# Folding the inverse transform of modes 0 to 31 into x early, and running the rest of the inverse on row halves

## The chip, the cores and the metric

The kernel runs on one core of a Trainium2 chip. The metric is device time in microseconds (us) of one execution. In its first measurement the kernel before took 431.39 us (median of 3 runs, 431.38 to 431.8).

## The reference, cut to what matters

```python
# linear attention, elu+1 features; x is (8, 576, 512)
x = attention(q, k, v)
X = rfft(x, axis=1)[:, :64]                     # 64 modes
Yr = Xr @ w_r[m] - Xi @ w_i[m]                  # per mode m: two 512x512 weight matrices
Yi = Xr @ w_i[m] + Xi @ w_r[m]
u = x + irfft(Y, n=576, axis=1)
out = u + relu(u @ w_ch)
```

The weights are 128 matrices of 1 MB (float32). They are cast to bfloat16 while they are loaded, so 512 KB of each lands on the chip. Because of the relu no row of the output can be finished before the last mode is known.

## The kernel before

After the attention, the kernel streams the weights through eight buffers and multiplies mode by mode. Between the modes it computes `x @ w_ch` for 36 tiles of 128 rows (`E0`). Near the end it turns the mode results `YT` into rows: for each batch entry `b`, `YZ[b]` holds the 112 rows of modes 0 to 55 (real and imaginary), once as they are (half 0) and once multiplied by `w_ch` (half 1).

```python
def form_rows(b):                       # called for two b after each of modes 55 to 58
    for ec in range(NDC):
        nc.tensor.matmul(z_ps[: 2 * NE, :], lhs[ec], wch16[:, ec, :], start=..., stop=...)
    for ec in range(NDC):
        nc.tensor.transpose(y_ps[: 2 * NE, ec, :], lhs[ec], id16)
    ...                                 # copied to YZ[b][:112, 1], YZ[b][:112, 0]

# mode_product(kk), kk >= 60: fillers keep TensorE busy
    if t == 1 and kk >= NM - 4: keep_warm(6)      # between the w_r and the w_i product
    if NM - 4 <= kk < NM - 1:   keep_warm(3)      # twice more; last_mode has keep_warm(3)

# the rows of modes 56 to 63 come last: one tile `last`, copied into each YZ[b] by DMA
for b in (1, 2, 3, 4, 5, 6, 7, 0):
    eng = nc.sync if b in (1, 2) else nc.gpsimd
    eng.dma_start(out=YZ[b][2 * NE : 128, :, :], in_=last[b::B, :, :])
```

The last stage works on 18 pairs of tiles. For each pair `channels` copies `E0` into PSUM (where the results of matmuls add up) with an identity matmul, `rectified` adds the inverse of half 1 and applies relu on ScalarE, and `finish` adds the inverse of half 0, after which VectorE adds x and sync issues the store. Each of these steps is one 512-column matmul per tile, six per pair, and the inverse contracts over all 128 rows (64 modes times two):

```python
mm(acc[r, :], inv_sb[:, sel], YZ[b][:, half, :])
...
for n in range(4, len(pairs)):
    channels(n); rectified(n); finish(n - 1)
```

## Time and profile before

| | before |
|---|---|
| time, median of 3 | 431.39 us |
| span of the profiled execution, first to last instruction | 429.8 us |
| last product of the last mode ends | 395.65 us |
| first store issued | 400.34 us |
| last VectorE add ends | 424.57 us |

The page of the kernel before, its busy times and three of its rows in 40 slices (each slice is 10.7 us):

```profile
PE 296.9 (69%) x2551; PEld 154.8 (36%) x2551; DVE 181.9 (42%) x373; ACT 146.6 (34%) x227; POOL 91.5 (21%) x165
...
PEclk9999666565558765566556678555658655999998
DMA  8999999999999999999999999999999999995697
GB/s 148 207 208 209 209 210 210 211 214 215 222 211 214 215 213 214 214 214 214 213 213 214 214 213 214 213 214 214 213 213 214 214 214 214 214 213 97 239 369 296
```

The DMA row is at 9 in nearly every slice. The bytes per second are those written on chip or to memory, near 213 GB/s while the weights stream. The windows view of the kernel before follows; its columns are the stretch in us, its length, the busy time of each engine with the number of instructions, the granted TensorE clock, the mean share of the 16 DMA engines, and GB/s:

```profile
core 0: us, PE busy (x) PEld busy (x) DVE busy (x) ACT busy (x) POOL busy (x), PEclk, DMA share, GB/s
300.00:350.00 50.00, 35.85 (x260) 14.13 (x259) 14.86 (x40) 12.31 (x22) 11.09 (x21) 0.64 1.06 213
...
390.00:395.00 5.00, 4.95 (x44) 2.23 (x44) 1.31 (x2) 0.00 (x0) 0.00 (x0) 1.00 0.41 76
...
400.00:404.00 4.00, 3.81 (x18) 1.79 (x17) 3.04 (x4) 2.40 (x6) 1.03 (x3) 1.00 0.63 222
404.00:408.00 4.00, 4.00 (x23) 1.96 (x22) 3.79 (x4) 3.20 (x7) 0.00 (x0) 1.00 0.89 359
408.00:412.00 4.00, 4.00 (x20) 1.68 (x20) 3.31 (x4) 2.98 (x7) 0.00 (x0) 1.00 0.91 370
412.00:416.00 4.00, 4.00 (x20) 2.05 (x19) 3.79 (x4) 3.33 (x7) 0.00 (x0) 1.00 0.98 382
...
420.00:424.00 4.00, 2.75 (x14) 0.85 (x12) 3.41 (x5) 2.04 (x4) 0.00 (x0) 1.00 1.02 408
424.00:428.00 4.00, 0.00 (x0) 0.00 (x0) 0.57 (x1) 0.00 (x0) 0.00 (x0) 0.71 0.81 297
```

In the weight phase the DMA share is 1.06 and TensorE is 72% busy. From 390 us the stream runs out. In the tail, 404 to 420 us, TensorE is busy for 4.00 of 4.00 us, VectorE for 3.3 to 3.8, and the stores move 359 to 382 GB/s. One pair of tiles in the timeline of the kernel before (start, length, engine, line, operation, count):

```profile
415.03 0.59 PE L593 MATMUL acc<-E,id 128*128 128x512 f16 x2
...
415.46 1.03 PE L549 MATMUL acc<-YZ,inv_sb 128*128 128x512 f16 x4
415.88 1.07 ACT L604 ACTIVATE acc<-acc 128x512 f32<-128x512 f32 x2 [0.22 <-PE acc L549]
...
416.32 0.59 PE L593 MATMUL acc<-E,id 128*128 128x512 f16 x2
```

From one pair to the next it is 1.29 us, six matmuls of 0.216 us. Line 593 is `channels`, line 549 the inverse, line 604 the relu.

### The profile page before, as it was taken

The page shows a single profiled execution, that of the slowest core. Times are in us where ns is not written, and L with a number is a line of the kernel's source. Part 1 is how long each engine was busy: PE and PEld are TensorE (multiplying, and loading weights), DVE is VectorE, ACT ScalarE, POOL GpSimd, SP SyncE. Part 2 cuts the span into 40 slices and gives each one's busy share as a digit, 9 for nine tenths or more (in the row PEclk, how much of TensorE's full clock was granted, in tenths as well). Part 3 has the DMA queues.
Part 4 walks back from the last instruction along what each step waited for, and adds up shares of the span by engine and source line. Part 5 has one row for each costly group of instructions (what it writes and reads, how often), then busy time and mean ns, then how long its engine had stood idle before and what let it go on. Part 6 is the DMA issues. An engine that isn't in the chain of part 4 may idle for free.

```text
span 429.8 us, 6238 instructions
## 1 busy us (share of the span) xinstructions
PE 296.9 (69%) x2551; PEld 154.8 (36%) x2551; DVE 181.9 (42%) x373; ACT 146.6 (34%) x227; POOL 91.5 (21%) x165
## 2 busy tenths in 40 slices
PE   0358776887018776856886666778675758999993
PEld 0346555664003332322232222322222324954441
DVE  1699998955004233233232322332323322211694
ACT  3687666631002222222222322122212222311782
POOL 4232223222102312121112221221211121110200
PEclk9999666565558765566556678555658655999998
DMA  8999999999999999999999999999999999995697
GB/s 148 207 208 209 209 210 210 211 214 215 222 211 214 215 213 214 214 214 214 213 213 214 214 213 214 213 214 214 213 213 214 214 214 214 214 213 97 239 369 296
DMA packets 35803, 92.38 MB, mean 215 GB/s; under 512 B 3136, under 2 KB 16448, under 8 KB 35776
## 3 DMA queue, kind: packets, MB, share of 16 engines
q0 software_dynamic: 32000, 82.00, 98.2%
q1 hardware_dynamic: 3776, 10.00, 6.1%
q8 instruction: 20, 0.33, 0.3%
q14 instruction: 7, 0.06, 0.0%
HBM read 164.07 MB, written 9.44 MB: 404 GB/s over the span
## 4 chain that ended last, share of the span: by engine, by line
DMA 67%; PE 17%; issue 7%; DVE 4%; ACT 2%; POOL 1%; DVEq 0%; POOLq 0%; ACTq 0%
DMA wi<-in_moe_w_i_dram 33%; DMA wr<-in_moe_w_r_dram 22%; DMA k<-in_k_dram 11%; PE acc L549 4%; PE P L355 3%; PE z L530 2%; PE zl L340 2%; PE acc L593 2%; PE eps L507 2%; PE yp L534 1%; DVE x L272 1%; ACT ke L187 1%; DVE k L194 0%; ACT qT L223 0%; POOL q L169 0%
## 5 line engine op out<-in xcount | busy, mean ns | idle before, releaser
L507 PE MATMUL eps<-wch,xTw 128*128 128x512 f16 x144 | 62.3, 582 | 3.4 <-DVE xTw L504 3.1
L515 ACT CAST E<-eps 128x512 f16<-128x512 f32 (+1 forms) x40 | 21.3, 543 | 122.7 <-PE eps L507 122.7
L115 POOL DMA_DIRECT2D wr<-in_moe_w_r_dram x64 | 34.0, 531 | 135.5 <-PE P L355 109.4
L355 PE MATMUL P<-wi,xt_c 128*32 128x512 bf16 x252 | 42.1, 565 | 27.3 <-DMA wi<-in_moe_w_i_dram 27.3
L355 PE MATMUL P<-wr,xt_c 128*32 128x512 bf16 x252 | 42.6, 582 | 22.9 <-DMA wr<-in_moe_w_r_dram 20.9
L115 POOL DMA_DIRECT2D wi<-in_moe_w_i_dram x65 | 34.5, 531 | 108.5 <-PE P L355 74.1
L355 PEld LDWEIGHTS <-xt_c 128*32 128x32 bf16 x504 | 24.3, 163 | 67.8 <-issue 38.7
L369 DVE CAST ys<-P 128x512 f16<-128x512 f32 x32 | 22.0, 688 | 59.7 <-PE P L355 59.7
L151 PEld LDWEIGHTS <-qT 64*128 64x128 f16 (+1 forms) x640 | 21.5, 126 | 56.8 <-issue 41.8
L371 ACT CAST ys<-P 128x512 f16<-128x512 f32 x31 | 18.1, 585 | 63.2 <-PE P L355 63.0
L373 PE MATMUL yt<-pick_sb,ys 128*128 128x16 f16 x252 | 16.8, 177 | 31.6 <-DMA pick_sb<-row_pick 20.4
L504 DVE COPY xTw<-xTp 128x512 f16<-128x512 f16 x36 | 15.2, 423 | 51.8 <-PE xTp L502 51.8
L373 PEld LDWEIGHTS <-ys 128*128 128x128 f16 x252 | 12.3, 105 | 51.1 <-issue 23.4
L151 PE MATMUL num<-kv,qT 64*128 64x65 f16 (+1 forms) x320 | 14.0, 230 | 22.6 <-ACT kv L247 20.1
L507 PEld LDWEIGHTS <-xTw 128*128 128x128 f16 x144 | 14.7, 124 | 33.7 <-issue 24.2
L492 DVE TENSOR_TENSOR x_main<-nw,rd 128x256 f32<-128x256 f32 x32 | 12.1, 419 | 33.8 <-PE nw L151 33.7
L187 ACT ACTIVATE qe<-q 128x1152 f16<-128x1152 f16 x16 | 17.7, 1155 | 22.9 <-DMA q<-in_q_dram 22.9
L216 PE MATMUL qTp<-id,qe 128*128 128x128 f16 x144 | 16.6, 310 | 12.1 <-DVE qe L200 11.7
L499 ACT CAST x16w<-x_main 128x512 f16<-128x512 f32 x32 | 19.8, 619 | 14.2 <-DVE x_main L492 14.2
L272 DVE TENSOR_TENSOR x<-num,rd 128x512 f16<-128x512 f32 x32 | 22.1, 691 | 1.1
L491 DVE RECIPROCAL rdw<-nw 128x4 f32<-128x4 f32 (+1 forms) x40 | 5.5, 170 | 38.3 <-PE nw L151 38.2
L502 PE MATMUL xTp<-id,x16w 128*128 128x128 f16 x144 | 19.4, 278 | 2.8 <-ACT x16w L499 2.4
(71 smaller groups left out, 413.7 us busy)
## 6 DMA issues: line engine op xcount, KB each, us to landing
wr<-in_moe_w_r_dram POOLq DMA_DIRECT2D x64, 512.0 KB, 18.6
wi<-in_moe_w_i_dram POOLq DMA_DIRECT2D x63, 512.0 KB, 18.6
out_dram<-x_main SPq DMA_DIRECT2D x14, 512.0 KB, 3.1
q<-in_q_dram POOLq DMA_DIRECT2D x8, 576.0 KB, 13.5
k<-in_k_dram POOLq DMA_DIRECT2D x8, 576.0 KB, 14.7
v<-in_v_dram POOLq DMA_DIRECT2D x8, 576.0 KB, 16.9
out_dram<-x_main SPq DMA_DIRECT2D x4, 256.0 KB, 3.4
out_dram<-x_tail SPq DMA_DIRECT2D x2, 512.0 KB, 3.4
```

Of the source, the lines that this page charges most:

```text
L115: tc.keep_in_program_order(nc.gpsimd.dma_start(out=w[:, dcs], in_=rows_of[:, dcs, :]))
L151: mm = nc.tensor.matmul(num[hpo][orow, c0 : c0 + 65], qT[rows, hpp, h2, cols], kv_sb[rows, hpp, h2, :])
L187: pin(nc.scalar.activation(out=ev[:, c], in_=heads(nm, b)[:, c], func=AF.Exp))
L272: nc.vector.tensor_tensor(out=dst.rearrange("p (o c d) -> p o c d", o=2, c=4), in0=nv[:, :, :, 0:64], in1=rden.unsqueeze(3).broadcast_to([ ...
L355: mm = nc.tensor.matmul(P[i][dc * 32 : dc * 32 + 32, :], xt_cols(dc, t, kk), w[:, dc, i * pw : i * pw + pw], start=(t == 1), stop=(t == 0) ...
L369: nc.vector.tensor_copy(out=dst, in_=P[i])
L371: nc.scalar.copy(out=dst, in_=P[i])
L373: mm = nc.tensor.matmul(yt_ps[:, ec, kk % 8, :], st[:, ec * 128 : ec * 128 + 128], pick_sb)
L499: nc.scalar.copy(out=x16, in_=x)
L502: nc.tensor.transpose(xT_ps[:, c, :], x16[:, c * 128 : c * 128 + 128], id16)
L507: nc.tensor.matmul(e_ps, xT[:, c, :], wch16[:, c, :], start=(c == 0), stop=(c == NDC - 1))
L515: nc.scalar.copy(out=dst, in_=e_ps[:, cols])
```

## The change

Its intent is to take a third of TensorE's work out of the last stage. The inverse of modes 0 to 31 is added to x earlier, in modes 32 to 55, before `x @ w_ch` is computed. So the last stage has only modes 32 to 63 to add, 64 rows instead of 128. These 64 rows are kept twice, in rows 0 to 63 and in rows 64 to 127, so that the two tiles of a pair can use different row halves of the array at the same time. The rows of modes 56 to 63 must then be copied into both halves: sixteen small DMA copies instead of eight. One constant that was loaded (144 KB) is built on the chip instead. The fillers of the last modes were set anew. The core of the diff:

```diff
+    FILL = {61: (2, 2, 1), 62: (5, 3, 3), 63: (6,)}
...
-            if t == 1 and kk >= NM - 4:
-                keep_warm(6)
-        if NM - 4 <= kk < NM - 1:
-            keep_warm(3)
+            if t == 1:
+                work_slot(kk, 0)
+                keep_warm(fill[0])
...
-    nc.sync.dma_start(out=inv0_sb, in_=inv0_dr.ap())
 (inv0_sb and inv2_sb, which holds modes 32 to 63 in both row halves, are built by selection matmuls)
...
+    def fold(t: int):                  # modes 32 to 55, pinned, with turn_x and channel_product
+                    acc[orow, :], inv_sb[: 2 * NF, rows_of(jj, BASE[b % 2])], YE[b][: 2 * NF, :]
+        pin(nc.vector.tensor_tensor(out=x, in0=acc, in1=x, op=ALU.add))
...
+    def form_z(b: int):                # spread over modes 56 to 60; form_y likewise
+            for h in range(2):
+                        z_ps[HALVES[h], :], yt, wch16[:, ec, :],
...
+                if n < N_PRE:
+                    mm(i, orow, inv0_sb[:, sel_rows], last[:, half, :])
+                else:
+                    g = HALVES[i]
+                    mm(i, orow, inv2_sb[g, sel_rows], YZ[b][g, half, :])
...
-        eng.dma_start(out=YZ[b][2 * NE : 128, :, :], in_=last[b::B, :, :])
+        for h in range(2):
+            eng.dma_start(out=YZ[b][64 * h + 48 : 64 * h + 64, :, :], in_=last[b::B, :, :])
```

More of the change, by code (lines that the diff above doesn't have):

```diff
@@ L18, with _dft_consts @@
 NP = 64
-def _dft_consts(S: int, NM: int, NL: int, NB: int):
+def _dft_consts(S: int, NM: int):
     m = np.arange(NM)
@@ L37, in _dft_consts @@
             pick[quad * 32 + c, c] = 1.0
-    inv0 = np.zeros((NL, 2, NB, S), dtype=np.float64)
-    inv0[:, :, 0, :] = inv[NM - NL :]
-    return (
-        fwd.astype(np.float16), inv.reshape(2 * NM, S).astype(np.float16),
-        inv0.reshape(2 * NL * NB, S).astype(np.float16), pick,
-    )
+    return fwd.astype(np.float16), inv.reshape(2 * NM, S).astype(np.float16), pick
 @with_exitstack
@@ L70 @@
     NE = NM - NL
-    fwd_np, inv_np, inv0_np, pick_np = _dft_consts(S, NM, NL, B)
+    NF = NM // 2
+    fwd_np, inv_np, pick_np = _dft_consts(S, NM)
     id16_dr = nc.inline_tensor(np.eye(128, dtype=np.float16), name="ident16")
@@ L75 @@
     inv_dr = nc.inline_tensor(inv_np, name="dft_inv")
-    inv0_dr = nc.inline_tensor(inv0_np, name="dft_inv_first")
     pick_dr = nc.inline_tensor(pick_np, name="row_pick")
@@ L345, in mode_product @@
         st = stage.tile([128, D], F16, tag="ystage", bufs=2, name=f"ys{kk}")
-        n_part = 1
-        pw = D // n_part
-        P = [
-            ps.tile([128, D], F32, tag="P", bufs=2, name=f"P{kk}_{i}")[:, 0:pw] for i in range(n_part)
-        ]
-        for t, w in ((1, wr), (0, wi)):
-            for i in range(n_part):
-                for dc in range(NDC):
-                    mm = nc.tensor.matmul(
-                        P[i][dc * 32 : dc * 32 + 32, :], xt_cols(dc, t, kk),
-                        w[:, dc, i * pw : i * pw + pw],
+        fixed = pin if kk >= NF else (lambda ins: ins)
@@ L358, in mode_product @@
+        fill = FILL.get(kk, (0, 0, 0))
+        P = ps.tile([128, D], F32, tag="P", bufs=2, name=f"P{kk}")
+        for t, w in ((1, wr), (0, wi)):
+            for dc in range(NDC):
+                fixed(
+                    nc.tensor.matmul(
+                        P[dc * 32 : dc * 32 + 32, :], xt_cols(dc, t, kk), w[:, dc, :],
                         start=(t == 1), stop=(t == 0), tile_position=(0, dc * 32),
                     )
-                    if kk >= NM - 4:
-                        pin(mm)
@@ L362, in mode_product @@
-            if t == 1 and kk >= NM - 4:
-                keep_warm(6)
-        if NM - 4 <= kk < NM - 1:
-            keep_warm(3)
-        for i in range(n_part):
-            dst = st[:, i * pw : i * pw + pw]
-            if (kk + i) % 2 == 0:
-                nc.vector.tensor_copy(out=dst, in_=P[i])
-            else:
-                nc.scalar.copy(out=dst, in_=P[i])
+                )
+            if t == 1:
+                work_slot(kk, 0)
+                keep_warm(fill[0])
+        if kk % 2 == 0:
+            fixed(nc.vector.tensor_copy(out=st, in_=P))
+        else:
+            fixed(nc.scalar.copy(out=st, in_=P))
@@ L372, in mode_product @@
+        work_slot(kk, 1)
+        keep_warm(fill[1])
         for ec in range(NDC):
-            mm = nc.tensor.matmul(
-                yt_ps[:, ec, kk % 8, :], st[:, ec * 128 : ec * 128 + 128], pick_sb
-            )
-            if kk >= NM - 4:
-                pin(mm)
-        if NM - 4 <= kk < NM - 1:
-            keep_warm(3)
+            fixed(
+                nc.tensor.matmul(
+                    yt_ps[:, ec, kk % 8, :], st[:, ec * 128 : ec * 128 + 128], pick_sb
+                )
+            )
@@ L381, in last_mode, with work_slot @@
+        keep_warm(fill[2])
+    work: list = []
+    per_slot: dict[int, list] = {}
+    def work_slot(kk: int, slot: int):
+        for _ in range(per_slot[kk][slot] if kk in per_slot else 0):
+            if work:
+                work.pop(0)()
     def last_mode(ps):
@@ L400, in last_mode @@
         product(1, wr, range(NDC))
-        keep_warm(3)
+        keep_warm(FILL[kk][0])
         product(0, wi, range(3))
@@ L421 @@
     inv_sb = ystage.tile([2 * NM, S], F16, name="inv_sb")
+    inv2_sb = ystage.tile([128, S], F16, name="inv2_sb")
     inv0_sb = ystage.tile([128, S], F16, name="inv0_sb")
+    sel = ystage.tile([128, 2, 128], F16, name="row_sel")
     nc.sync.dma_start(out=inv_sb, in_=inv_dr.ap())
-    nc.sync.dma_start(out=inv0_sb, in_=inv0_dr.ap())
+    nc.vector.memset(sel, 0.0)
+    for h in range(2):
+        nc.vector.tensor_copy(out=sel[:, 0, h * 64 : h * 64 + 64], in_=id16[:, 2 * NF : 128])
+    nc.vector.tensor_copy(out=sel[:, 1, 0:128:B], in_=id16[:, 2 * NE : 128])
     YT = ystage.tile([128, NDC, NM, 2 * B], F16, name="YT")
+    nc.vector.memset(YT[:, :, NE:NM, :], 0.0)
     yt_ps = None
@@ L436, in mode @@
         if kk == NM - 2:
-            nc.vector.tensor_copy(out=YT[:, :, NE : NM - 1, :], in_=yt_ps[:, :, 0 : NL - 1, :])
+            pin(nc.vector.tensor_copy(out=YT[:, :, NE : NM - 1, :], in_=yt_ps[:, :, 0 : NL - 1, :]))
         elif kk % 8 == 7:
-            nc.vector.tensor_copy(out=YT[:, :, kk - 7 : kk + 1, :], in_=yt_ps)
+            ins = nc.vector.tensor_copy(out=YT[:, :, kk - 7 : kk + 1, :], in_=yt_ps)
+            if kk >= NF:
+                pin(ins)
     for kk in range(n_early):
@@ L450 @@
     YZ = [sW.tile([128, 2, D], F16, tag="YZ", bufs=B, name=f"YZ{b}") for b in range(B)]
+    YE: dict[int, object] = {}
     E0: dict[int, object] = {}
@@ L473, with parts_of, attention_rows @@
     last_ps = []
-    def channel_product(t: int):
-        num = [bank(f"nw{t}_{o}") for o in range(2)]
-        tail = t >= B * NJJ
-        if tail:
-            i = t - B * NJJ
-            parts = [(2 * i + h, NJJ, slice(h * 64, h * 64 + 64)) for h in range(2)]
-        else:
-            parts = [(t // NJJ, t % NJJ, slice(0, 128))]
+    for i, dst in enumerate((inv2_sb, inv0_sb)):
+        for cols in (slice(0, 512), slice(512, S)):
+            r_ps = bank(f"rows{i}_{cols.start}")[:, 0 : cols.stop - cols.start]
+            nc.tensor.matmul(r_ps, sel[:, i, :], inv_sb[:, cols])
+            nc.scalar.copy(out=dst[:, cols], in_=r_ps)
+    def parts_of(t: int):
+        if t < B * NJJ:
+            b, jj = divmod(t, NJJ)
+            return [(b, jj, slice(0, 128))]
+        p = t - B * NJJ
+        return [(2 * p + h, NJJ, HALVES[h]) for h in range(2)]
+    def attention_rows(t: int):
+        num = [bank(f"nw{t}_{o}") for o in range(2)]
         x = x_of(t)
-        for b, jj, orow in parts:
+        for b, jj, orow in parts_of(t):
             nv = num_matmuls(num, orow, q_view(qT_all[b]), kv_all[b], rows_of(jj, BASE[b % 2]))
@@ L494, in channel_product, with early_rows @@
                     in0=nv[o][:, :, 0:64],
-                    in1=rden.unsqueeze(2).broadcast_to([64 if tail else 128, 4, Dh]),
+                    in1=rden.unsqueeze(2).broadcast_to([orow.stop - orow.start, 4, Dh]),
                     op=ALU.mult,
                 )
-        x16 = sW.tile([128, D], F16, tag="x16w", bufs=2, name=f"x16w{t}")
-        nc.scalar.copy(out=x16, in_=x)
+    def early_rows(b: int):
+        r = 2 * NF
+        y_ps = bank(f"ye{b}", [128, NDC, 128], F16)
+        for ec in range(NDC):
+            yt = YT[:, ec, 0:NF, :].rearrange("p m (t b) -> p (m t) b", b=B)[:, :, b]
+            pin(nc.tensor.transpose(y_ps[:r, ec, :], yt, id16))
+        YE[b] = sW.tile([128, D], F16, tag="YE", bufs=2, name=f"YE{b}")
+        pin(nc.vector.tensor_copy(out=YE[b][:r], in_=y_ps[:r].rearrange("p c r -> p (c r)")))
@@ new lines @@
+    x16w, xTw = {}, {}
+    def fold(t: int):
+        x = x_of(t)
+        acc = bank(f"ya{t}")
+        for b, jj, orow in parts_of(t):
+            pin(
+                nc.tensor.matmul(
+                    acc[orow, :], inv_sb[: 2 * NF, rows_of(jj, BASE[b % 2])], YE[b][: 2 * NF, :]
+                )
+            )
+        pin(nc.vector.tensor_tensor(out=x, in0=acc, in1=x, op=ALU.add))
+        x16w[t] = sW.tile([128, D], F16, tag="x16w", bufs=2, name=f"x16w{t}")
+        pin(nc.scalar.copy(out=x16w[t], in_=x))
@@ L500, in channel_product, with turn_x @@
+    def turn_x(t: int):
+        x16 = x16w.pop(t)
         xT_ps = bank(f"xTp{t}", [128, NDC, 128], F16)
         for c in range(NDC):
-            nc.tensor.transpose(xT_ps[:, c, :], x16[:, c * 128 : c * 128 + 128], id16)
-        xT = sW.tile([128, NDC, 128], F16, tag="xTw", bufs=2, name=f"xTw{t}")
-        nc.vector.tensor_copy(out=xT, in_=xT_ps)
+            pin(nc.tensor.transpose(xT_ps[:, c, :], x16[:, c * 128 : c * 128 + 128], id16))
+        xTw[t] = sW.tile([128, NDC, 128], F16, tag="xTw", bufs=2, name=f"xTw{t}")
+        pin(nc.vector.tensor_copy(out=xTw[t], in_=xT_ps))
@@ L505, in channel_product @@
+    def channel_product(t: int):
+        xT = xTw.pop(t)
         e_ps = bank(f"eps{t}")
         for c in range(NDC):
-            nc.tensor.matmul(
-                e_ps, xT[:, c, :], wch16[:, c, :], start=(c == 0), stop=(c == NDC - 1)
-            )
-        need = {t // NJJ} if not tail else {2 * i, 2 * i + 1}
-        for b in sorted(need):
+            pin(
+                nc.tensor.matmul(
+                    e_ps, xT[:, c, :], wch16[:, c, :], start=(c == 0), stop=(c == NDC - 1)
+                )
+            )
+        for b, _, _ in parts_of(t):
@@ L514, in channel_product @@
         for cols, dst in e0_parts(t):
-            nc.scalar.copy(out=dst, in_=e_ps[:, cols])
+            pin(nc.scalar.copy(out=dst, in_=e_ps[:, cols]))
     tiles = []
@@ L520 @@
         tiles += [(2 * i + 1) * NJJ + jj for jj in range(NJJ)]
-    def form_rows(b: int):
+    def form_z(b: int):
         z_ps = bank(f"z{b}")
+        for ec in range(NDC):
+            yt = YT[:, ec, NF:NM, :].rearrange("p m (t b) -> p (m t) b", b=B)[:, :, b]
+            for h in range(2):
+                pin(
+                    nc.tensor.matmul(
+                        z_ps[HALVES[h], :], yt, wch16[:, ec, :],
+                        start=(ec == 0), stop=(ec == NDC - 1), skip_group_check=True,
+                    )
+                )
+        pin(nc.scalar.copy(out=YZ[b][:, 1, :], in_=z_ps))
@@ L525, in form_rows, with form_y @@
+    def form_y(b: int):
         y_ps = bank(f"yp{b}", [128, NDC, 128], F16)
-        lhs = [
-            YT[:, ec, 0:NE, :].rearrange("p m (t b) -> p (m t) b", b=B)[:, :, b] for ec in range(NDC)
-        ]
         for ec in range(NDC):
+            yt = YT[:, ec, NF:NM, :].rearrange("p m (t b) -> p (m t) b", b=B)[:, :, b]
+            for h in range(2):
+                pin(nc.tensor.transpose(y_ps[HALVES[h], ec, :], yt, id16))
+        pin(nc.vector.tensor_copy(out=YZ[b][:, 0, :], in_=y_ps.rearrange("p c r -> p (c r)")))
@@ L530, in form_rows, with fold_first @@
+    def fold_first(t: int):
+        x = x_of(t)
+        acc = bank(f"yb{t}")
+        pin(
             nc.tensor.matmul(
-                z_ps[: 2 * NE, :], lhs[ec], wch16[:, ec, :], start=(ec == 0), stop=(ec == NDC - 1)
+                acc, inv2_sb[0 : 2 * NF, rows_of(t % NJJ, BASE[0])], YZ[0][0 : 2 * NF, 0, :]
             )
-        for ec in range(NDC):
-            nc.tensor.transpose(y_ps[: 2 * NE, ec, :], lhs[ec], id16)
-        nc.scalar.copy(out=YZ[b][: 2 * NE, 1, :], in_=z_ps[: 2 * NE, :])
@@ L536, in form_rows @@
-        nc.vector.tensor_copy(
-            out=YZ[b][: 2 * NE, 0, :], in_=y_ps[: 2 * NE].rearrange("p c r -> p (c r)")
         )
+        pin(nc.vector.tensor_tensor(out=x, in0=acc, in1=x, op=ALU.add))
     last = sW.tile([128, 2, D], F16, tag="last", bufs=1, name="last")
-    EARLY, LATE, BOTH = 1, 2, 3
-    def add_inverse(n: int, i: int, t: int, half: int, what: int = BOTH):
-        acc = accs[n][:, i]
-        mm = lambda o, l, r: on_bank(
-            n, {i}, nc.tensor.matmul(o, l, r, start=False, stop=True, skip_group_check=True)
-        )
-        if t < B * NJJ:
-            b, jj = divmod(t, NJJ)
-            parts = [(b, slice(0, 128), rows_of(jj, BASE[b % 2]))]
-        else:
-            p = t - B * NJJ
-            parts = [
-                (2 * p + h, slice(h * 64, h * 64 + 64), rows_of(NJJ, BASE[h])) for h in range(2)
-            ]
-        for b, r, sel in parts:
-            if what == BOTH:
-                mm(acc[r, :], inv_sb[:, sel], YZ[b][:, half, :])
-                continue
-            if what & EARLY:
-                mm(acc[r, :], inv_sb[: 2 * NE, sel], YZ[b][: 2 * NE, half, :])
-            if what & LATE:
-                mm(acc[r, :], inv0_sb[:, sel], last[:, half, :])
@@ new lines, in add_inverse, with mm @@
+    def add_inverse(n: int, half: int):
+        def mm(i, orow, l, r):
+            on_bank(
+                n, {i},
+                nc.tensor.matmul(
+                    accs[n][orow, i], l, r, start=False, stop=True, skip_group_check=True
+                ),
+            )
+        for i, t in enumerate(pairs[n]):
+            for b, jj, orow in parts_of(t):
+                sel_rows = rows_of(jj, BASE[b % 2])
+                if n < N_PRE:
+                    mm(i, orow, inv0_sb[:, sel_rows], last[:, half, :])
+                else:
+                    g = HALVES[i]
+                    mm(i, orow, inv2_sb[g, sel_rows], YZ[b][g, half, :])
@@ L599, in rectified @@
     def rectified(n: int):
-        for i, t in enumerate(pairs[n]):
-            add_inverse(n, i, t, 1, LATE if n < N_PRE else BOTH)
+        add_inverse(n, 1)
         for i in range(2):
@@ L624, in finish @@
         t0 = pairs[n][0]
+        add_inverse(n, 0)
         for i, t in enumerate(pairs[n]):
-            if n < N_PRE:
-                add_inverse(n, i, t, 0, EARLY)
-                add_inverse(n, i, t, 0, LATE)
-            else:
-                add_inverse(n, i, t, 0)
             if single:
@@ L639, in finish, with spread, first_rows, rows_ahead @@
         store(t0, 2)
-    done = 0
-    rows_done = 0
-    n_spread = NE - 4 - n_early
+    def spread(n_items: int, step: int, steps: int):
+        return range(n_items * step // steps, n_items * (step + 1) // steps)
+    def first_rows(n: int, i: int):
+        on_bank(
+            n, {i},
+            nc.tensor.matmul(
+                accs[n][:, i], inv2_sb[0 : 2 * NF, rows_of(pairs[n][i] % NJJ, BASE[0])],
+                YZ[0][0 : 2 * NF, 1, :], start=False, stop=False, skip_group_check=True,
+            ),
+        )
+    last_ps.append(psW.tile([128, D], F32, tag="zl", bufs=1, name="zl0"))
+    made: set = set()
+    def rows_ahead(t: int):
+        for b, _, _ in parts_of(t):
+            if b not in made:
+                made.add(b)
+                work.append(lambda b=b: early_rows(b))
+    rows_ahead(tiles[0])
+    for u in range(-2, len(tiles)):
+        if u + 3 < len(tiles):
+            rows_ahead(tiles[u + 3])
+        for stage, k in ((fold, u + 2), (turn_x, u + 1), (channel_product, u)):
+            if 0 <= k < len(tiles):
+                work.append(lambda stage=stage, t=tiles[k]: stage(t))
+    n_fold = len(work)
+    for b in range(B):
+        work.append(lambda b=b: form_z(b))
+        work.append(lambda b=b: form_y(b))
+        if b == 0:
+            work += [lambda t=t: fold_first(t) for t in range(NJJ)]
+    n_form = len(work) - n_fold
+    for kk in range(NF, NE):
+        per_slot[kk] = [len(spread(n_fold, 2 * (kk - NF) + s, 2 * (NE - NF))) for s in range(2)]
+    for kk in range(NE, NE + 5):
+        per_slot[kk] = [len(spread(n_form, 2 * (kk - NE) + s, 10)) for s in range(2)]
     for kk in range(n_early, NM):
         mode(kk)
-        want = min(len(tiles), (kk - n_early + 1) * len(tiles) // n_spread)
-        while done < want:
-            channel_product(tiles[done])
-            done += 1
-        if kk >= NE - 1:
-            while rows_done < min(B, 2 * (kk - NE + 2)):
-                form_rows(rows_done)
-                rows_done += 1
-        if kk == NM - 5:
+        if kk < NF:
+            for i in spread(len(tiles), kk - n_early, NF - n_early):
+                attention_rows(tiles[i])
+        if kk == NE + 4:
+            assert not work
             psB.release()
@@ L658 @@
             )
+            per_slot[NE + 5] = [N_PRE, N_PRE]
             for n in range(N_PRE):
-                channels(n)
-                for i, t in enumerate(pairs[n]):
-                    add_inverse(n, i, t, 1, EARLY)
-            last_ps.append(psW.tile([128, D], F32, tag="zl", bufs=1, name="zl0"))
+                work.append(lambda n=n: channels(n))
+                work.append(lambda n=n: [first_rows(n, i) for i in range(2)])
     last_ps.append(psW.tile([128, D], F32, tag="P", bufs=2, name="zl1"))
@@ L687 @@
         eng = nc.sync if b in (1, 2) else nc.gpsimd
-        eng.dma_start(out=YZ[b][2 * NE : 128, :, :], in_=last[b::B, :, :])
+        for h in range(2):
+            eng.dma_start(out=YZ[b][64 * h + 48 : 64 * h + 64, :, :], in_=last[b::B, :, :])
     psW.release()
```

## The prediction

> **What bounds the kernel now.** Until 394.5 us it is the weight stream. The windows view gives 213–214 GB/s at a DMA share of 1.06 in every stretch from 100 to 385 us; a weight load takes 18.6 us to land, about the eight buffers in flight, so TensorE may lag many microseconds without starving it. TensorE is 72% busy there at a granted clock near 0.6, waiting for weights. The last bytes land at 394–395 us, the last product ends at 395.6, the first store is issued at 400.3, data flows until 427.2, and the span ends at 429.8. In this tail (timeline, 404–419 us) TensorE is back to back: six 512-column matmuls at 0.216 us make 1.293 us per pair of tiles. VectorE's add takes 1.224 us of that, ScalarE's two relus 0.99 us start to start. A pair stores 512 KB, and 512 KB per 1.293 us is 405 GB/s: the windows show 401–407 GB/s at a share of 1.00–1.04 when undisturbed. So TensorE, VectorE and the stores are nearly level.
>
> **What the change does.**
> - Fold phase: 36 more 512-column matmuls, 32 more transposes, 36 more VectorE adds' worth of movement (x needs one PSUM add of about 0.69 us per tile, against none before), all in modes 32–55, about 118 us of stream. At full clock I count 80 us of TensorE work there, at half clock 137. It will run short of time when cold, then be continuously busy and warm: it follows the stream with a lag of a few us, which eight buffers hide. Off the path.
> - Form phase (modes 56–60, 24.6 us): 64-column halves written twice. The trace's strided weight loads (290 ns for 112 columns) suggest 2–2.7 us per batch entry instead of 1.7: TensorE about full, lag up to 3 us, recovered in modes 61–62 because fillers fall from 12 per mode to 5 and 11.
> - Stream: one 144 KB constant less: 0.3–0.7 us.
> - Tail: the two matmuls of a step use row halves and different banks. The trace's 64-row attention matmuls start 4 ns apart in such pairs, so I expect 4 slots instead of 6. The Trainium skill, "TensorEngine Tiling (Array Packing)", Key Properties, says that a change of tiling mode drains the array; here the 64-column tail pair shows about 0.1 us at each switch. So TensorE needs about 1.08 us per pair, with the wait for relu about 1.18, VectorE 1.14–1.22. The stores then bind: 1.25–1.3 us per pair. The steady pace hardly gains; what is gained is the slack: the 1.54 us of the two tail pairs, the slow start (272 GB/s at 403–405 us), the dips to 330 GB/s. 16 pairs at about 410 GB/s (estimate from 401–407 seen) from 404 us end near 424.5–425.5 instead of 427.2.
> - Sixteen small row copies instead of eight: sync issues four by about 400.1 and gpsimd twelve at 0.49 us each until 404; the last lands near 406.5, just before the tile that needs it (about 407).
>
> **Sum:** 0.5 (stream) + 0.3 (first pair needs one matmul less per tile) + 2.0 (tail) = 2.8 us less: **428.6 us**, range 427.0 to 430.6. Chances: faster by over 2% 0.02, within 2% 0.95, slower 0.03.
>
> **Right if** the profile shows the stream still at 213 GB/s, ending near 394 us; half matmuls starting within 10 ns of each other; TensorE with gaps in the tail; DMA share at 1.0 or more from 404 us to the end; steps of 1.25–1.3 us between stores. **Wrong if** row halves run one after the other (tail as before), if the stores have more headroom (pace 1.2, about 427), if TensorE reaches mode 63 late because the pinned order makes it wait on VectorE or ScalarE while cold (slower), or if the later row copies stall the third or seventh pair.

## The result, and the profile after

The changed kernel took 429.78 us (median of 4 runs, 429.39 to 430.25), the kernel before beside it 431.44 us. The ratio is 0.996 with a 95% interval of 0.9943 to 0.9978. Here and below a ratio is the mean time of one kernel's runs over that of the other's of the same rounds, so it is not quite the ratio of the medians quoted. Executions over 1.5% slower than the fastest of the same kernel are left out of the means. A second set of 5 runs gave 429.62 us and 0.9957. The change is worth 1.7 to 2.0 us. The predicted 428.6 us was 1.2 us too low, within the range of 427.0 to 430.6.

The page of the changed kernel:

```profile
PE 275.9 (64%) x2674; PEld 157.4 (37%) x2674; DVE 208.6 (49%) x426; ACT 149.2 (35%) x231; POOL 94.5 (22%) x171
...
PEclk9999865667558755555555599988999999699996
DMA  8999999999999999999999999999999999995697
```

The DMA row is as full as before. From the middle of the span on, where the fold begins, the clock row is mostly at 9. The busy share of TensorE hardly tells of it: from 300 to 350 us it is 35.85 of 50 us at a granted clock of 0.64 before, and 36.86 of 50 us at 1.00 after (the first lines of the two tables of windows). The same windows of the changed kernel:

```profile
core 0: us, PE busy (x) PEld busy (x) DVE busy (x) ACT busy (x) POOL busy (x), PEclk, DMA share, GB/s
300.00:350.00 50.00, 36.86 (x280) 19.53 (x280) 21.54 (x41) 22.12 (x39) 10.64 (x22) 1.00 1.06 214
...
390.00:395.00 5.00, 4.22 (x49) 2.02 (x48) 1.37 (x3) 0.00 (x0) 0.00 (x0) 1.00 0.34 64
...
400.00:404.00 4.00, 3.80 (x19) 0.74 (x15) 3.26 (x4) 3.62 (x8) 2.83 (x6) 1.00 0.86 297
404.00:408.00 4.00, 3.79 (x28) 1.25 (x26) 3.68 (x4) 3.30 (x7) 0.00 (x0) 1.00 1.00 389
408.00:412.00 4.00, 4.00 (x23) 0.91 (x22) 4.00 (x4) 3.50 (x7) 0.00 (x0) 1.00 1.02 402
412.00:416.00 4.00, 4.00 (x22) 0.93 (x21) 4.00 (x5) 3.57 (x7) 0.00 (x0) 1.00 1.04 409
...
420.00:424.00 4.00, 0.00 (x0) 0.00 (x0) 0.90 (x2) 0.00 (x0) 0.00 (x0) 0.72 1.02 396
424.00:428.00 4.00, 0.00 (x0) 0.00 (x0) 0.00 (x0) 0.00 (x0) 0.00 (x0) 0.50 0.37 140
```

In the tail, from 408 to 416 us, VectorE is now busy 4.00 of 4.00 us, its adds following each other without a gap. From 404 to 424 us the DMA engines move 389 to 409 GB/s at a share of 1.00 to 1.04; the first of these windows holds the last row copies too. VectorE is done by 421 us, but the DMA engines work on for another 4 to 6 us: the 140 GB/s from 424 to 428 us are 0.56 MB, 1.4 us at 400 GB/s, and the last packet comes at 426.84 us. The same pair of the tail in the changed kernel:

```profile
411.04 0.60 PE L649 MATMUL acc<-E,id 128*128 128x512 f16 x2
...
411.58 0.75 PE L610 MATMUL acc<-YZ,inv_sb 64*128 64x512 f16 x4
...
412.26 0.60 PE L649 MATMUL acc<-E,id 128*128 128x512 f16 x2
```

The first two of the four half matmuls (line 610) start 4 ns apart in this trace, so they do run side by side. From the start of the four to the next line it takes 0.68 us instead of 0.86 (411.58 to 412.26, and 415.46 to 416.32 before): two slots of 0.216 us, a wait of about 0.13 us for the second relu, and a switch. The pace is 1.20 us per pair instead of 1.29 (1.19 and 1.22 in turn). Between the start of the first line and that of the second lie 0.54 us, where two matmuls take 0.43: the remaining 0.11 us is the switch from the full array to row halves. With full rows in the same kernel (an experiment below) these two lines start 0.43 to 0.44 us apart. The Trainium skill, "TensorEngine Tiling (Array Packing)", Key Properties, says that changing the tiling mode drains the array; this trace agrees and puts about 0.1 us on each switch.

What became of the stores is told by their landing. These are lines of the DMA issues, KB each and the median time from issue to landing; first the kernel before, then the changed one:

```profile
out_dram<-x_main SPq DMA_DIRECT2D x14, 512.0 KB, 3.1
```

```profile
out_dram<-x_main SPq DMA_DIRECT2D x14, 512.0 KB, 4.6
```

A store takes 1.5 us longer to land. The experiment with half the stores, below, shows that it queues behind others: there the time to landing falls to 2.5 to 3.8 us for all but the first three stores. The milestones, read from the traces (us; the last weight packet is from the trace's DMA packet records, the last product is where VectorE's copy of it starts):

| profiled execution | last weight packet | last product | first add | first store | last add ends | span | first add to span's end |
|---|---|---|---|---|---|---|---|
| before | 394.17 | 395.68 | 399.62 | 400.34 | 424.57 | 429.77 | 30.15 |
| changed | 393.97 | 394.61 | 398.20 | 399.34 | 420.90 | 428.39 | 30.19 |
| changed, second | 393.41 | 394.06 | 397.65 | 398.79 | 420.40 | 427.65 | 30.00 |

So VectorE finished 3.7 us earlier, and of these 1.4 us were there before the first add. The stage that the change was made for, from its first add to the end, is as long as before.

### The profile page after: what moved, and what is told of

The parts are those of the page before. It is cut to its first block, busy times and chain, and to the rows that moved or that the text cites. A ratio compares the mean times of both kernels' runs of the same rounds, so it can differ in the third digit from the quotient of the medians.

```text
span 428.4 us, 6567 instructions
## 1 busy us (share of the span) xinstructions
PE 275.9 (64%) x2674; PEld 157.4 (37%) x2674; DVE 208.6 (49%) x426; ACT 149.2 (35%) x231; POOL 94.5 (22%) x171
## 4 chain that ended last, share of the span: by engine, by line
DMA 78%; PE 6%; DVE 6%; issue 5%; POOL 2%; ACT 1%; DVEq 0%; POOLq 0%
DMA wi<-in_moe_w_i_dram 61%; DMA wr<-in_moe_w_r_dram 5%; DMA pick_sb<-row_pick 4%; DMA q<-in_q_dram 4%; DMA k<-in_k_dram 4%; PE P L349 2%; DVE x L267 2%; PE acc L610 2%; PE acc L649 1%; POOL YZ L772 1%; DMA YZ<-last 1%; DVE qe L195 1%; ACT ke L182 1%; DVE q L189 1%; DVE rd L264 0%
## 5 line engine op out<-in xcount | busy, mean ns | idle before, releaser
L349 PE MATMUL P<-wi,xt_c 128*32 128x512 bf16 x252 | 36.5, 518 | 45.3 <-DMA wi<-in_moe_w_i_dram 45.3
L349 PEld LDWEIGHTS <-xt_c 128*32 128x32 bf16 x504 | 30.0, 153 | 83.7 <-issue 72.6
L349 PE MATMUL P<-wr,xt_c 128*32 128x512 bf16 x252 | 36.8, 523 | 26.1 <-DMA wr<-in_moe_w_r_dram 24.0
L535 DVE TENSOR_TENSOR x_main<-ya,x_main 128x512 f32<-128x512 f32 x32 | 22.1, 691 | 42.5 <-PE ya L531 42.5
L554 PE MATMUL eps<-wch,xTw 128*128 128x512 f16 x144 | 39.6, 401 | 0.0
L146 PEld LDWEIGHTS <-qT 64*128 64x128 f16 (+1 forms) x640 | 23.5, 125 | 39.6 <-issue 18.9
L146 PE MATMUL nw<-kv,qT 64*128 64x65 f16 (+1 forms) x320 | 20.0, 235 | 1.4 <-DVE x_tail L506 1.0
L659 ACT ACTIVATE acc<-acc 128x512 f32<-128x512 f32 x36 | 19.1, 581 | 3.2 <-PE acc L610 0.9
L211 PEld LDWEIGHTS <-qe 128*128 128x128 f16 x144 | 14.7, 147 | 13.4 <-DVE qe L195 12.1
L182 ACT ACTIVATE ke<-k 128x1152 f16<-128x1152 f16 x16 | 17.7, 1155 | 4.9 <-DMA k<-in_k_dram 4.9
```

The costliest lines, as they stand in the source:

```text
L146: mm = nc.tensor.matmul(num[hpo][orow, c0 : c0 + 65], qT[rows, hpp, h2, cols], kv_sb[rows, hpp, h2, :])
L182: pin(nc.scalar.activation(out=ev[:, c], in_=heads(nm, b)[:, c], func=AF.Exp))
L211: nc.tensor.transpose(qT_ps[:, j].rearrange("p t r -> p (t r)"), phi["q", b][:, hpp, j].rearrange("p o d -> p (o d)"), id16,)
L349: nc.tensor.matmul(P[dc * 32 : dc * 32 + 32, :], xt_cols(dc, t, kk), w[:, dc, :], start=(t == 1), stop=(t == 0), tile_position=(0, dc * 32),)
L535: pin(nc.vector.tensor_tensor(out=x, in0=acc, in1=x, op=ALU.add))
L554: nc.tensor.matmul(e_ps, xT[:, c, :], wch16[:, c, :], start=(c == 0), stop=(c == NDC - 1))
```

## The experiments

Two theories about the tail were tested. Theory A: in the changed kernel the stores and row copies share a DMA limit near 400 GB/s, so a faster TensorE only lengthens the queue of stores. Theory B: the pace of TensorE and VectorE sets the end. Each batch ran on one chip together with the kernel before.

### The changed kernel again

> The changed kernel, not edited, as the measure for the other runs of this batch. Expected 429.4 to 430.3 us, ratio to the kernel before 0.995 to 0.997.

429.62 us (429.37 to 429.92), kernel before 431.55, ratio 0.9957 (0.9944 to 0.9969). As expected.

### Full rows in the last stage

```diff
-    for h in range(2):
-        nc.vector.tensor_copy(out=sel[:, 0, h * 64 : h * 64 + 64], in_=id16[:, 2 * NF : 128])
+    nc.vector.tensor_copy(out=sel[:, 0, 0:64], in_=id16[:, 2 * NF : 128])
-                    g = HALVES[i]
-                    mm(i, orow, inv2_sb[g, sel_rows], YZ[b][g, half, :])
+                    mm(i, orow, inv2_sb[:, sel_rows], YZ[b][:, half, :])
```

> The changed kernel, but in the last stage the inverse uses all 128 rows with the second half of its matrix zero, so the two matmuls of a step run one after the other (0.216 us each, 1.29 us per pair) and no tiling mode is switched, except in the two pairs of row tails. Same result. Theory A (the stores and the small row copies share a DMA limit near 400 GB/s, so a faster TensorE only makes a longer queue of stores): the last VectorE add moves from 420.9 to about 423.5 us, the last store lands less late after it, and the time rises by only 0 to 0.8 us. Theory B (the pace of TensorE and VectorE sets the end): 16 pairs times 0.085 us plus 0.5 for the tails, about 1.9 us more, 431.6 us.

430.49 us, ratio 0.9977 (0.9964 to 0.9989), right result: 0.9 us slower than the changed kernel in the same batch. In the traces the last add ends at 422.87 us instead of 420.40, 2.5 us later, while the span grew by 0.2 us in the profiled pair and by 0.9 us in the medians. Its windows in the tail:

```profile
412.00:416.00 4.00, 4.00 (x20) 2.02 (x19) 3.79 (x4) 3.33 (x8) 0.00 (x0) 1.00 1.02 408
...
420.00:424.00 4.00, 1.06 (x6) 0.15 (x2) 2.60 (x4) 0.68 (x2) 0.00 (x0) 1.00 0.93 366
```

TensorE is back at 4.00 of 4.00 us, and yet the stores move as much from 412 to 416 us as with row halves (408 and 409 GB/s). Theory A expected up to 0.8 us, theory B 1.9 us; the measurement is next to A. The row halves by themselves are worth at most about 0.9 us. Full rows also pay for the copies once more: TensorE's first step of the third pair, which now reads both halves of the rows at once, waits for a row copy at 399.29 us, and the third add starts 1.19 us after the second ends, where it is 0.69 us in the changed kernel.

### Without the copies to the second half

```diff
-        for h in range(2):
+        for h in range(1):
             eng.dma_start(out=YZ[b][64 * h + 48 : 64 * h + 64, :, :], in_=last[b::B, :, :])
```

> The changed kernel without the eight row copies to the second half (wrong result on purpose: modes 56 to 63 are missing in every second tile). 256 KB less move between 397 and 405 us. Theory A: 256 KB at about 400 GB/s is 0.65 us, so 0.4 to 0.8 us faster than the changed kernel, with VectorE ending at about the same time or a little earlier. Theory B: the copies are off the path but for one wait of 0.2 us; 0 to 0.3 us faster.

428.94 us, ratio 0.9943 (0.993 to 0.9955): 0.7 us faster than the changed kernel (medians; 0.6 by means). The result was meant to be wrong, but the check passed it as correct: it did not notice that modes 56 to 63 are missing in every second tile, so a "right result" in this study means only that this check passed. The gain is in A's range and above B's, though the five runs a side give it a 95% interval of 0.2 to 1.0 us, so this run alone does not exclude B. The edit takes away two costs at once. One is 256 KB of DMA traffic. The other is that sync issues two copies ahead of the first store instead of four, at 0.58 us each. From the start of the first add to the first store issue it is 0.72 us here, and 1.14 us in the changed kernel. The wait for a late copy at 405.5 us, 0.2 us, goes with them. The run doesn't tell these apart.

### Half the stores, in both kernels

```diff
         on_bank(n, {0, 1}, nc.vector.tensor_tensor(out=x, in0=acc, in1=x, op=ALU.add))
-        store(t0, 2)
+        if n % 2 == 1:
+            store(t0, 2)
```

> The changed kernel storing only every second pair of tiles (wrong result on purpose: half the output is never written). Theory A: the last data now land about 2.5 us after the last VectorE add instead of 4.5, so about 2 us faster, near 427.5 us, with the adds at the same pace as before. Theory B: no change beyond 0.5 us, as the adds still end near 420.9.

> The kernel before storing only every second pair (wrong result on purpose: half the output is never written). Theory A: here TensorE, not the stores, paces the tail; the last data land 3.0 to 3.6 us after the last add, and fewer stores can only take away the short queue at the end: 0.5 to 1.5 us faster, far from the 3.4 us of the changed kernel. If the stores bind here too, about 3 us faster.

The changed kernel with half the stores took 426.19 us, 3.4 us less than the whole one in the same batch. The kernel before with half the stores took 430.35 us, 1.45 us less than its own 431.8 us. (Both leave 8 of the 18 pairs unwritten, so their results are wrong; the first and the last pair are stored in any case.) The windows of the changed kernel, first with all stores, then with half of them:

```profile
404.00:420.00 16.00, 14.35 (x84) 3.90 (x80) 15.56 (x15) 12.86 (x24) 0.00 (x0) 1.00 1.02 405
420.00:424.00 4.00, 0.00 (x0) 0.00 (x0) 0.40 (x1) 0.00 (x0) 0.00 (x0) 0.74 1.02 393
```

```profile
404.00:420.00 16.00, 14.17 (x82) 3.87 (x80) 15.68 (x15) 12.74 (x24) 0.00 (x0) 1.00 0.57 227
420.00:424.00 4.00, 0.00 (x0) 0.00 (x0) 0.10 (x1) 0.00 (x0) 0.00 (x0) 0.69 0.37 131
```

VectorE is busy for the same 15.6 us of 16 and its last add ends at 420.40 and 420.10 us, so nothing upstream of the stores changed; only DMA traffic fell, from 405 to 227 GB/s. The end came 3.4 us earlier. Theory B is out. One rival inside theory A is left: with all stores, the time that sync takes to issue one grows from 0.33 us to as much as 1.29 us; with half of them it stays at 0.33 to 0.39 us after the first, and this run takes away issues and traffic together. The DMA share of 1.02 speaks for the traffic; it was not tested apart. My expectation of 2 us was too small: I had counted from 4.5 us between the last add and the last data, but from the last add to the span's end it is 7.25 us in the changed kernel and 4.0 us with half the stores. The two runs side by side also show what the stores hide: with half of them the changed kernel leads the kernel before by about 3.6 us (the ratios, 0.9879 and 0.9963, come from two chips) instead of 1.7 to 2.0, and its tail from the first add to the end is 26.72 us instead of 28.98.

### Full rows with eight copies

```diff
 (full rows, and)
-        for h in range(2):
+        for h in range(1):
```

> The run with full rows (no row halves at work) without the eight copies to the second half, which it doesn't need. Right result. Theory A: the copies take DMA time here too, but TensorE paces the tail, so only part of the 0.65 us comes back: 0.2 to 0.7 us faster than with full rows, 429.8 to 430.3 us, level with the changed kernel.

429.29 us, ratio 0.994 (0.9927 to 0.9953), right result. This kernel makes no use of row halves, and it is at least level with the changed kernel (0.9957, on another chip; the intervals overlap). What the halves gain in the tail and what their extra copies cost cancel. It was faster than expected by 0.5 us. The traces show where: the wait for the row copy in the third pair is gone, VectorE's idle time there falls from 1.19 us with full rows and sixteen copies to 0.58 us, and from the first add to the end it takes 29.67 us instead of 30.17. I had not counted this wait.

### Where the earlier start comes from: the fillers

In the profiled pair 1.1 us were gained before the last product. The timeline of the kernel before in modes 62 and 63; a bracket at the end of a line would tell an idle time and what ended it:

```profile
390.06 0.47 PE L355 MATMUL P<-wr,xt_c 128*32 128x512 bf16 x4
...
390.46 1.47 PE L340 MATMUL zl<-wch,id 128*128 128x512 f16 x6
...
391.86 0.47 PE L355 MATMUL P<-wi,xt_c 128*32 128x512 bf16 x4
...
393.89 0.64 PE L393 MATMUL y_last<-xt_c,wr 128*128 128x16 bf16 x16
...
394.36 0.81 PE L340 MATMUL zl<-wch,id 128*128 128x512 f16 x3
...
395.01 0.64 PE L393 MATMUL y_last<-xt_c,wi 128*128 128x16 bf16 x16
```

Nothing waits for a weight DMA: TensorE (line 340 is the fillers) is behind the stream. It got behind in the burst of `form_rows` from 362 to 379 us, and twelve fillers per mode left it little room to catch up: a mode with them takes it 3.87 us (386.19 to 390.06), against 4.9 us of stream per mode (1.05 MB at 213 GB/s). The changed kernel:

```profile
391.83 0.65 PE L391 MATMUL y_last<-xt_c,wr 128*128 128x16 bf16 x16 [0.34 <-DMA wr<-in_moe_w_r_dram]
...
392.32 1.46 PE L335 MATMUL zl<-wch,id 128*128 128x512 f16 x6
393.67 0.41 PEld L391 LDWEIGHTS <-wi 128*128 128x128 bf16 x12 [0.39 <-DMA wi<-in_moe_w_i_dram]
393.67 0.90 PE L391 MATMUL y_last<-xt_c,wi 128*128 128x16 bf16 x16
394.28 0.17 PEld L391 LDWEIGHTS <-wi 128*128 128x128 bf16 x4 [0.20 <-DMA wi<-in_moe_w_i_dram]
```

Here both halves of the last mode wait for their weights, so the product ends as soon as the stream allows. Two experiments changed only the fillers, the first in the kernel before:

```diff
-            if t == 1 and kk >= NM - 4:
-                keep_warm(6)
-        if NM - 4 <= kk < NM - 1:
-            keep_warm(3)
+            if t == 1:
+                keep_warm(FILL.get(kk, (0, 0, 0))[0])
+        keep_warm(FILL.get(kk, (0, 0, 0))[1])
 (and so at the other two places, FILL as in the changed kernel)
```

> The kernel before with the changed kernel's fillers in modes 60 to 63 (none in 60, 5 in 61, 11 in 62, 6 in 63, instead of 12, 12, 12 and 3). If the earlier end of the last product (394.0 to 394.6 us instead of 395.65) comes from the fillers, TensorE stops lagging behind the weights here too: the last product ends within 0.7 us of the last weight bytes instead of 1.5, and the time falls by 0.6 to 1.0 us. If it comes from the spread of the row forming or from the missing constant, nothing changes beyond 0.3 us.

Four of five runs took 430.99 to 431.49 us, ratio 0.9985 (0.9971 to 0.9999). The fifth, which was the profiled one, took 469.25 us and is left out: wherever its matmuls follow back to back, TensorE ran at half its rate (see the last section). So it was run again:

> The kernel before with the new fillers once more, as the profiled execution of the first run fell in a state where TensorE ran at half rate from start to end. Expected, if the fillers made TensorE late: last product within 0.7 us of the last weight bytes (1.5 to 1.7 with the old fillers), 0.5 to 0.9 us faster than the kernel before. If not: less than 0.3 us.

430.99 us, kernel before 431.56, ratio 0.9982 (0.997 to 0.9994), which is 0.6 to 0.8 us. Its timeline:

```profile
391.94 0.65 PE L393 MATMUL y_last<-xt_c,wr 128*128 128x16 bf16 x16 [0.27 <-DMA wr<-in_moe_w_r_dram]
...
393.75 0.93 PE L393 MATMUL y_last<-xt_c,wi 128*128 128x16 bf16 x16
```

TensorE now waits for the weights of mode 63, and the last product comes 0.64 us after the last weight packet (394.08, 394.72) instead of 1.5. So the fillers alone, without any other part of the change, give about a third to two fifths of its gain. The second experiment gave the changed kernel the old fillers, but for the twelve of mode 60:

```diff
-    FILL = {61: (2, 2, 1), 62: (5, 3, 3), 63: (6,)}
+    FILL = {61: (6, 3, 3), 62: (6, 3, 3), 63: (3,)}
```

> The changed kernel with the fillers of the kernel before in its last modes (12, 12 and 3 in modes 61, 62 and 63 instead of 5, 11 and 6). If the fillers alone decide, the last product ends 0.5 us or more later after the last weights and the time rises by 0.5 us. If TensorE lagged in the kernel before because the forming of rows came in one burst at modes 55 to 58, which the change spreads over modes 56 to 60, then TensorE waits for weights in modes 61 to 63 anyway and the old fillers fit in: less than 0.3 us.

429.63 us, ratio 0.9953 (0.9941 to 0.9965): no change. TensorE isn't late, and the old fillers fit into its waits; it still waits for the last weights, and the last product comes 0.63 us after the last weight packet:

```profile
393.00 0.89 PE L391 MATMUL y_last<-xt_c,wi 128*128 128x16 bf16 x16 [0.54 <-DMA wi<-in_moe_w_i_dram]
```

So either remedy takes the lag away: fewer fillers in the kernel before, or the rest of the change. That it is the spread of the row forming, and not another part of the change or mode 60 without fillers, is likely but not shown: no run varied it alone.

### Versions meant to beat both

The first keeps row halves for batch entries 1 to 3 only. Entries 4 to 7 use full rows with zeros in the second half, so they need one copy, and sync issues two copies instead of four:

```diff
+    NH = B // 2
+    for b in range(NH, B):
+        nc.vector.memset(YZ[b][64:128, :, :], 0.0)
-                    g = HALVES[i]
+                    g = HALVES[i] if b < NH else slice(0, 128)
-    for b in (1, 2, 3, 4, 5, 6, 7, 0):
-        eng = nc.sync if b in (1, 2) else nc.gpsimd
-        for h in range(2):
+    for b in (1, 2, 3, 0, 4, 5, 6, 7):
+        for h in range(2 if 0 < b < NH else 1):
+            eng = nc.sync if (b, h) in ((1, 0), (2, 0)) else nc.gpsimd
 (form_z and form_y write the second half for b < NH alone)
```

> A version meant to beat both: row halves only for batch entries 1 to 3, full rows with a zero second half for entries 4 to 7, so that 11 row copies remain of 16, two of them on sync instead of four, so the first store isn't issued behind four copies (0.45 us late in the changed kernel). Right result. Theory A: 160 KB less at 400 GB/s is 0.4 us and the earlier first store up to 0.4 us; 0.3 to 0.8 us faster than the changed kernel, 428.8 to 429.4 us. Theory B (the pace of TensorE and VectorE binds): full rows for half the pairs cost about 0.9 us, 430.5 us.

428.86 us, ratio 0.9928 (0.9916 to 0.9941), right result. It was repeated as a measure for the next version:

> The version with eleven row copies once more, on the chip of the next run, as its measure: ratio to the kernel before 0.992 to 0.9945.

428.32 us, ratio 0.9923 (0.991 to 0.9936). This is the fastest version by a clear distance from the changed kernel: 3.1 to 3.3 us less than the kernel before, by means. It was made slower on TensorE in half of the pairs and won, which B excludes. Its windows of the tail:

```profile
400.00:404.00 4.00, 3.94 (x21) 0.92 (x21) 3.48 (x3) 3.39 (x8) 0.58 (x2) 1.00 0.96 355
404.00:408.00 4.00, 4.00 (x26) 1.39 (x25) 3.84 (x5) 3.71 (x8) 0.00 (x0) 1.00 1.01 406
...
424.00:428.00 4.00, 0.00 (x0) 0.00 (x0) 0.00 (x0) 0.00 (x0) 0.00 (x0) 0.50 0.01 4
```

From 400 to 404 us it moves 355 GB/s where the changed kernel moves 297, and there is next to nothing left after 424 us, where the changed kernel still moves 0.56 MB.

The second version also brings the third pair's add forward:

```diff
+        for zy in ((slice(1, 2), slice(0, 1)) if b == 1 else (slice(0, 2),)):
-                eng.dma_start(out=YZ[b][64 * h + 48 : 64 * h + 64, :, :], in_=last[b::B, :, :])
+                eng.dma_start(out=YZ[b][64 * h + 48 : 64 * h + 64, zy, :], in_=last[b::B, zy, :])
     finish(0)
-    channels(3)
+    rectified(2)
     finish(1)
-    rectified(2)
+    channels(3)
     rectified(3)
```

> The version with eleven copies, with the two copies for entry 1 split so that the rows of the channel product are copied as soon as they are there, about 0.35 us before the other rows, and with the third pair's first step issued before the second pair is finished, so that VectorE's idle 0.65 us before the third pair goes away. Right result. If the start of the stores still leaves DMA time unused (share 0.6 to 0.9 from 398 to 402 us), 0.3 to 0.6 us faster than with eleven copies; if not, no change.

428.33 us, ratio 0.992 (0.9907 to 0.9932): no change. VectorE's idle 0.64 us before the third pair did go away; the third add now follows the second without a gap, but the second came 0.2 us later, and the stores didn't gain.

## Why the prediction was right or wrong

The time was within the range, but the sum was near by luck: two errors of opposite sign met, a tail that gained nothing and an earlier start that was not foreseen. By its terms:

- "0.5 (stream)": the last weight packet comes at 393.4 us on average over ten fast traces of the changed kernel and its variants, and at 393.9 us over three of the kernel before and its variants. That is 0.6 us, near what was said, but the ranges overlap (393.1 to 394.0 and 393.5 to 394.2 us). That the missing constant is the cause was not tested by itself.
- "lag up to 3 us, recovered in modes 61–62": right for the changed kernel, but I overlooked that the kernel before was late itself, by 1.5 us from the last weight packet to the last product. The change takes 0.9 us of it away. I had read the chain at 394 us as weight-bound, though the timeline of the kernel before shows no wait for weights there. A run with only the fillers changed confirmed it (0.6 to 0.8 us).
- "0.3 (first pair)": from the last product to the first add it takes 3.59 us instead of 3.94. Right by size.
- "2.0 (tail)": this is the step that failed. From the first add to the end the tail takes 30.19 and 30.00 us in two traces of the changed kernel, 30.15 in the kernel before. The mechanism was right: halves side by side, a pace of 1.20 us (I said 1.18), stores that bind. What was mis-sized is what remains when stores bind. I counted 410 GB/s for the 16 remaining pairs; the windows show 389 to 409. And I treated the sixteen row copies as a matter of latency only ("the last lands near 406.5"; the wait came, 0.2 us at 405.5). They also use the DMA time that the stores lack, and four of them stand on sync's queue ahead of the first store. Taking eight away gave 0.6 to 0.7 us; taking the row halves away cost about 0.9 us. What the halves gain is nearly what their copies cost.
- The signs that I named: the stream, the half matmuls 3 to 4 ns apart and the DMA share came as said. The steps of 1.25 to 1.3 us between stores did not: sync issues them 1.19 to 1.25 us apart from 410 to 418 us, and TensorE shows no gap there by its busy time (4.00 of 4.00 us from 408 to 416 us). Stores that bind do not hold back the adds here; the queue grows instead, and what it holds is paid after the last add.
- My range for the end of the data (424.5 to 425.5 us) was met by the bulk of the bytes (near 425.4 us by the sum above), though not by the last packet (426.84 us, 428.16 before). But I booked all of it as gain of the tail, when 1.4 us of it came from an earlier start.
- Fold phase "off the path": right. The stream stays at 213 GB/s; TensorE was warm (granted clock 1.00 from 300 to 350 us) and not short of time; nor was it continuously busy, as I had said (36.86 of 50 us).
- Form phase "2–2.7 us per batch entry": wrong for six of eight entries, which took 1.5 us (379.88 to 381.37 us for one); the two from 365.4 to 370.9 us, where the granted clock was partly 0.5, took 2.3. In the example from 379.88 us the loads of the two column halves start 1 to 5 ns apart, and so do their matmuls, so writing the halves twice took no second turn. It was off the path.

What stays open: the exact split of the copies' cost between traffic, issue and waits, and why half of the last 128 packets of the stores are through 0.5 to 1.6 us before the last one in the fast traces.

## What to carry to other kernels

When engines and stores are nearly level, a faster engine buys a queue: ask of each stage what its bytes take at the rate seen, and count the small copies that the change adds among those bytes and in the issue queue. Before crediting a stage with an earlier end, subtract the earlier start. And where a stage is said to wait for data, look for that wait in the timeline: here TensorE was late by its own fillers after a burst of work, and taking that away in the kernel before gave a third to two fifths of what the whole restructuring gained.

## What the Trainium skill lacked or had wrong

- "TensorEngine Tiling (Array Packing)", Key Properties, says that a mode switch drains the array but gives no duration: about 0.1 us per switch here (start to start 0.31 us at a switch, in either direction, where it is 0.216 us without), two switches per pair, so that the four slots of 0.216 us of a pair take about 1.07 us by this sum.
- "DMA: Bandwidth & Descriptors", Where 436 GB/s comes from, says without a condition that the HBM side (about 358 GB/s) binds transfers between HBM and on-chip memory. Here a program on one core stored at 396 to 409 GB/s for 16 us (windows 408 to 424 us, no row copy under way), above that figure and below the 435 GB/s that the page gives as the fabric's ceiling. The page's own single-core figure for a load of 16 MB, 425 GB/s, fits better; that section gives about 358 GB/s only for two cores that stream at once.
- "TensorE: Matmul & The Clock Gate", HAM trace caveats, tells of a clock stuck low for over 50 us. One of the 5 runs of the kernel before with new fillers went further: 469.25 us, and TensorE at half rate even where it was busy for 20 and 40 us on end (360 to 380 and 410 to 450 us). Its trace holds no clock record at all: the page has no PEclk row, and the 1.00 that the views print is only what they print without records. Matmuls of 512 columns follow at 0.44 us instead of 0.216, as in this pair of its tail:

```profile
422.69 1.05 PE L593 MATMUL acc<-E,id 128*128 128x512 f16 x2
423.58 2.05 PE L549 MATMUL acc<-YZ,inv_sb 128*128 128x512 f16 x4
425.46 1.17 PE L593 MATMUL acc<-E,id 128*128 128x512 f16 x2
```

- No page found tells what small on-chip copies cost beside a saturated stream of stores: here eight copies of 32 KB, two of them issued by sync ahead of the first store, were worth 0.6 to 0.7 us.
